# Decode block, backward pass: slab products ordered behind store copies on VectorE, and the forward output stored in the last attention pass

## Chip, cores and metric

One NeuronCore of one Trainium2 chip runs the program; nothing is exchanged with other cores. The metric is the device time of one execution in microseconds (us): the median of three runs, with the lowest and the highest beside it. One further execution is recorded by the hardware profiler; every duration, wait and order below comes from it.

The engines are named as the profile names them: PE is TensorE (matmuls and transposes; PEld its weight loads), DVE is VectorE, ACT is ScalarE, POOL is GpSimd, SP is SyncE. In this kernel SP issues all loads from memory and POOL all stores. Each engine runs its own instruction stream in order.

## What is computed

The reference is a model of four layers applied to one token, and all its gradients. A is attention over a cache of 65,536 positions (32 query heads in 4 groups, head size 128), B a dense layer with a squared relu; both are applied twice with the same weights and the same cache:

```python
x = x + A(layernorm(x), k_cache, v_cache, wq, wo)     # L1
x = x + B(layernorm(x), w1, b1, w2, b2)               # L2
x = x + A(layernorm(x), k_cache, v_cache, wq, wo)     # L3
x = x + B(layernorm(x), w1, b1, w2, b2)               # L4
out, vjp = jax.vjp(f, A_x, A_k_cache, A_v_cache, A_wq, A_wo, B_w1, B_b1, B_w2, B_b2)
grads = vjp(grad_out)
return out, *grads
```

All data are bfloat16. K and V cache are 67 MB each (4 x 65,536 x 128), and so are their gradients. The ten outputs are the forward result `out_0` (1024 values), the gradient of x (`out_1`), of K and V (`out_2`, `out_3`), of wq, wo, w1, b1, w2, b2 (`out_4` to `out_9`).

## The kernel before

**Stages.** The cache is read four times. Pass 1 and pass 2 are the forward attention of L1 and L3 (`attn_fwd`), pass 3 is the first half of L3's backward attention (`attn_bwd3`, softmax gradient and the gradient of the queries), and pass 4, the last, is `attn_bwd4`: the backward attention of L1, and the K and V gradients of L1 and L3 together. Between the passes stand dense stages for the weights; the last of them, called dense34, runs after pass 3 with a PSUM layout of its own.

**The last pass.** `attn_bwd4` goes over 256 items of 8 x 128 cache rows, in 4 groups of 64. `pipeline` (L840) calls, item by item, the steps of the pass, each with its lag: `vT` turns 8 blocks of V on PE and evacuates them to `kt` (L1345, L1348), up to 16 items ahead; `vS` multiplies them with dO (L1382) and forms X on DVE (L1403); `eIn`, `eT` and `xT` turn the saved probabilities and X (L1354, L1360); `dV8` and `dK8` make rows of the V and K gradients; `k8` multiplies K by X for the query gradient (L1457). The K load of a block is written at its first use, the V load at its turn (`kv8`, L365).

**Store copies.** `dV8` and `dK8` call `outer16` (L1418): twice, two matmuls into `ps_gg` (two buffers; L1426), then an evacuation (`evac`, L1430) of 128 x 1024 numbers into a 1 MB staging slot. After two such calls the slot is stored by POOL (L1432). `evac` (L150) puts each copy on ACT (L161) or on DVE (L164), whichever has less written work by its own counts. These evacuations are the "store copies" of this text.

**Background work.** Each item ends with `bg.step` (L862), which advances one piece of other work. Two urgent kinds take the product of a weight matrix with a vector in row form, `g_dO` and `g_dn`, both through `g_rowdots` (L577). It goes over 8 slabs of 128 x 1024 numbers of wo or wq, loaded four at a time as one 1 MB slot (L462): for each slab, DVE multiplies the slab by a vector spread over all partitions (the slab product, L598, into one of the two buffers of `mv_t`), and one step later ACT sums the product along its rows (`total`, L587). Twelve such sets of four products fall into pass 4. The other kind, `bg.normal`, writes the weight gradients as outer products (`rank2`, L1504), paced by a count: a step is taken while the number done is under `bg.total` times the share of items gone. After three big outer products comes `g_biases`, which stores the gradients of b2 and b1.

**Slots.** Loads and staging share an arena of 20 slots of 1 MB, of which up to 8 hold saved probabilities until their group is done. Which slot each load gets is fixed as the program is written; the load then waits for the slot's last user.

**Order of the instructions.** Passes 1 to 3 are written under `tc.manual_schedule`: PE, DVE and ACT run in the text's order. Dense34 and pass 4 are not: there the planner of the framework orders each engine's stream at build time. It runs a model of the program, and each engine takes, of the instructions that are ready in that model, the one that is first in the text. An instruction whose inputs the model holds to be there early is thus put ahead of earlier-written ones that are not yet ready. The stream is then fixed, and on the chip an engine waits at each instruction until its inputs are there.

**The forward output.** In dense34 the second dense layer's w2 is gone through once for the gradient and, beside it (`side_x4`, L1849), for the forward result. After the last slab, `side_x4` adds the bias and the residual on DVE into `x4` (1024 values as 128 x 8) and calls `col_to_dram` (L202): a transpose to 8 rows on PE (L205), a copy to bfloat16 on DVE (L207), and a store of 2 KB issued by POOL (L208).

Of the kernel before, what the change touches and what calls it, by code (L numbers as in the profile page):

```python
# [3 lines left out]

# [9 lines left out]
ALU = mybir.AluOpType  # L14
# [6 lines left out]
def kernel(  # L21
# [24 lines left out]
    nc = tc.nc  # L46
    D = A_x.shape[-1]
    G = A_k_cache.shape[1]
# [3 lines left out]
    HQ = QD // DH  # L52
    R = HQ // G
    F = B_w1.shape[1]
    DC, FC = D // P, F // P
# [38 lines left out]
    def ps_gg():  # L94
        return PS["pool"].tile([P, 1024], F32, name="ps_gg", tag="gg", bufs=2)
# [4 lines left out]
    def ps_mv(shape, dtype=F32):  # L100
        if PS["pass4"]:
            return ps_tr(shape, dtype)
        return PS["pool"].tile(shape, dtype, name="ps_mv", tag="mv", bufs=1)
# [41 lines left out]
    def add_load(act=0.0, dve=0.0, pe=0.0):  # L145
        load["act"] += act
        load["dve"] += dve
        load["pe"] += pe

    def evac(out, in_, kind="bf"):  # L150
        n = 1
        for d in in_.shape[1:]:
            n *= d
        ca = 0.17 + n * 0.00083
        cd = 0.13 + n * (0.00105 if kind == "f32" else 0.00054)

        if PS["pass4"] and kind == "bf":
            ca += 1.5
        if kind == "kta" or kind != "kt" and load["act"] + ca <= load["dve"] + cd:
            load["act"] += 0.17 + n * 0.00083  # L160
            nc.scalar.copy(out=out, in_=in_)  # L161
        else:
            load["dve"] += cd
            nc.vector.tensor_copy(out=out, in_=in_)  # L164


    def col_from_dram(v1d, n, name):
        nj = n // P
        rows = tmp.tile([nj, P], BF, name="rows_c", tag="rows_c")
        nc.sync.dma_start(out=rows[:], in_=v1d.rearrange("(j p) -> j p", p=P))  # L170
        pt = ps_mv([P, nj], BF)
        nc.tensor.transpose(pt[:, :], rows[:, :], ident_b[0:nj, 0:nj])
        col = vec.tile([P, nj], F32, name=name)
        nc.vector.tensor_copy(out=col[:], in_=pt[:])
        return col
# [26 lines left out]
    def col_to_dram(col, n, v1d):  # L202
        nj = n // P
        pt = ps_mv([nj, P], F32)
        nc.tensor.transpose(pt[:, :], col[:, :], ident_f[:, :])  # L205
        rows = tmp.tile([nj, P], BF, name="rows_c", tag="rows_c")
        nc.vector.tensor_copy(out=rows[:], in_=pt[:])  # L207
        nc.gpsimd.dma_start(out=v1d.rearrange("(j p) -> j p", p=P), in_=rows[:])  # L208
# [227 lines left out]
    def d_cols(ap, nb):  # L436
        return ap[:, nb * P:(nb + 1) * P]
# [66 lines left out]
    def w2_slabs(ahead=1):  # L504
        v = f_rows_of(B_w2)
        return slabs("s_w2", lambda k, kn: v[:, k // 4, :, :], FC, 4, D, ahead)
# [52 lines left out]
    def g_bcast_vec(vcol, nj):  # L559
        pt = ps_mv([nj, P], F32)  # L560
        nc.tensor.transpose(pt[:, :], vcol, ident_f[:, :])
        yield
        rows = tmp.tile([32, P], BF, name="bc_rows")
        nc.vector.tensor_copy(out=rows[0:nj, :], in_=pt[:, :])
        vbc = mvs.tile([P, nj * P], BF, name="vbc", tag="vbc", bufs=1)
        yield
        for j0 in range(0, nj, 4):
            pg = ps_gg() if PS["pass4"] else ps_tr([P, 512], F32)
            for jj in range(4):
                nc.tensor.matmul(pg[:, jj * P:(jj + 1) * P], lhsT=ident_b[0:nj, j0 + jj:j0 + jj + 1].to_broadcast([nj, P]),  # L570
                                 rhs=rows[0:nj, :], start=True, stop=True)
            nc.scalar.copy(out=vbc[:, j0 * P:(j0 + 4) * P], in_=pg[:, 0:512])
            add_load(act=0.6)
            yield
        return vbc

    def g_rowdots(slab_it, nk, vcol, nj, finish, name):  # L577
        n = nj * P
        y = vec.tile([P, nk], F32, name=name)
        nc.gpsimd.memset(y[:], 0.0)  # L580
        vbc = None
        due = None
        steps = 8 if PS["pass4"] else WAIT_STEPS

        def total(t, kc):
            def f():
                nc.scalar.activation(out=t[:, :], in_=t[:, :], func=ACTF.Copy, accum_out=y[:, kc:kc + 1])  # L587
            return f
        for kc, slab in slab_it:
            if vbc is None:  # L590
                vbc = yield from g_bcast_vec(vcol, nj)
                for _ in range(steps - WAIT_STEPS + 1):
                    yield "wait"
            elif kc % 4 == 0:
                for _ in range(steps):
                    yield "wait"
            t = mvs.tile([P, n], BF, name="mv_t", tag="mv_t", bufs=2)
            nc.vector.tensor_tensor(out=t[:, :], in0=slab, in1=vbc[:, :], op=ALU.mult)  # L598
            add_load(dve=0.1 + n * 0.00054, act=0.42 + n * 0.00083)
            if due is not None:  # L600
                due()
            due = total(t, kc)
            yield
        due()
        yield
        r = finish(y[:, :])
        if r is not None:
            yield from r
        yield
# [382 lines left out]
    def g_dn(L, dn, g, first):  # L992
        yield from g_rowdots(wq_slabs(g)[0], DC, L["dqT"][:, gsl(g)], R, dn_finish(dn, first), "%s_dn%d" % (L["name"], g))
# [295 lines left out]
    def attn_bwd4(p, La, Lb, on_group, bg, stack, end=()):  # L1289
# [128 lines left out]
        def outer16(name, out, key, xt, gg, j1):  # L1418

            if j1 == 0:  # L1420
                state[key] = Slot(name, True)
            stg = state[key].t[:, :].rearrange("p (j d) -> p j d", d=DH)
            for m in range(2):
                pg = ps_gg()
                for h in range(2):
                    nc.tensor.matmul(pg[:, 512 * h:512 * h + 512], lhsT=xt[64 * h:64 * h + 64, j1 // 8 + m, :],  # L1426
                                     rhs=gg[64 * h:64 * h + 64, :, :].rearrange("p a b -> p (a b)"),
                                     start=True, stop=True, tile_position=(64 * h, 0))
                jj = j1 + 8 * m
                evac(stg[:, jj:jj + 8, :].rearrange("p j d -> p (j d)"), pg[:, :], kind="f32")  # L1430
            if j1 + 16 == J:
                nc.gpsimd.dma_start(out=out, in_=stg)  # L1432
                state.pop(key).free(stored=True)

        def dV8(g, c8):
            b, j0 = divmod(c8, J)
            if 2 * j0 < J:
                outer16("gstv", half(GVv, g, b), "stv", state[("xe", g, b)], state[("GG", g, c8 // SU)][1], 2 * j0)
# [131 lines left out]
    def n_outer(nA, nB, wide=False):  # L1570
        return -(-nB // 8) + nA // 4 + nA * (-(-nB // 8)) if wide else 1 + nA // 4 * 5
# [56 lines left out]
    bg = Background()  # L1628
# [39 lines left out]
    bg = Background()  # L1668
# [146 lines left out]
    bg = Background()  # L1815
# [30 lines left out]
    x4 = vec.tile([P, DC], F32, name="x4")  # L1846
    ps_x4 = ps_acc([P, DC, 64])

    def side_x4(kc, slab):  # L1849
        for nb in range(DC):  # L1850
            nc.tensor.matmul(ps_x4[:, nb, :], lhsT=d_cols(slab, nb), rhs=L4["gb"][:, kc:kc + 1].to_broadcast([P, 64]),
                             start=kc == 0 and nb == 0, stop=kc == FC - 1 and nb == DC - 1, skip_group_check=True)
        add_load(pe=DC * 0.03)
        if kc == FC - 1:
            f = tmp.tile([P, DC], F32, name="ffn_f")
            nc.vector.tensor_tensor(out=f[:], in0=ps_x4[:, :, 0], in1=b2c[:], op=ALU.add)
            nc.vector.tensor_tensor(out=x4[:], in0=x3[:], in1=f[:], op=ALU.add)
            col_to_dram(x4, D, out_0.rearrange("a b d -> (a b d)"))
    rows.add(w2_slabs()[0], FC, DC, lambda: dx2[:], fin_dh2, mix=True, side=side_x4)
    rows.add(w1_slabs()[0], DC, FC, lambda: dh2[:], fin_dx1, cols=f_cols, mix=True)  # L1860
    rows.add(wo_slabs(firstg[3])[0], R, DC, lambda: dx1[:], dO_finish(L1, firstg[3]), inplace=True)
# [10 lines left out]
    bg = Background()  # L1872
# [1 line left out]
    bg.normal.append(g_outer(bgpool, out_8, FC, DC, [L4["g"], L2["g"]], [gx, dx2], a_f=True))  # L1874
    bg.normal.append(g_outer(bgpool, out_5, HQ, DC, [L3["oT"], L1["oT"]], [dx3, dx1]))
    bg.normal.append(g_outer_wide(bgpool, out_6, DC, FC, [L4["n"], L2["n"]], [dh4, dh2]))
    bg.total = 2 + n_outer(FC, DC) + n_outer(DC, FC, True) + n_outer(HQ, DC) + (G - 1) * n_outer(DC, DC)
    bg.steps = len(ITEMS[3]) - 4
    dn1 = vec.tile([P, DC], F32, name="dn1")

    def g_biases():
        gb2 = tmp.tile([P, DC], F32, name="gb2")
        nc.vector.tensor_tensor(out=gb2[:], in0=gx[:], in1=dx2[:], op=ALU.add)
        col_to_dram(gb2, D, out_9)
        yield
        gb1 = tmp.tile([P, FC], F32, name="gb1")
        nc.vector.tensor_tensor(out=gb1[:], in0=dh4[:], in1=dh2[:], op=ALU.add)
        col_to_dram_f(gb1, F, out_7)
        yield
# [66 lines left out]
```

## Time and profile before

| | us |
|---|---|
| median of 3 runs (lowest to highest) | 1946.26 (1945.61 to 1947.33) |
| profiled execution, its own time | 1939.92 |
| its span | 1938.1 |
| PE busy / DVE busy / ACT busy in the span | 1585.2 / 1170.3 / 1044.9 |
| memory traffic: read, written | 617.62 MB, 165.69 MB, 404 GB/s over the span |

By stretches (from the windows of the trace; lengths and busy times in us; the DMA share is the mean busy share of the 16 DMA engines):

| stretch | what | PE | DVE | ACT | PEclk | DMA share | GB/s |
|---|---|---|---|---|---|---|---|
| 1110 to 1210 | dense34, start of pass 4 | 87.6 | 68.7 | 55.7 | 0.95 | 0.85 | 310 |
| 1210 to 1485 | pass 4 | 238.9 | 200.9 | 196.2 | 0.88 | 1.01 | 418 |
| 1485 to 1500 | pass 4 | 8.9 | 11.8 | 9.3 | 0.77 | 0.95 | 391 |
| 1500 to 1660 | pass 4 | 138.0 | 123.7 | 119.7 | 0.94 | 1.01 | 422 |
| 1660 to 1690 | pass 4 | 17.6 | 13.4 | 13.2 | 0.66 | 0.77 | 307 |
| 1690 to 1770 | pass 4 | 73.8 | 59.7 | 59.3 | 0.91 | 1.01 | 417 |
| 1770 to 1785 | pass 4 | 5.3 | 5.6 | 4.7 | 0.66 | 0.93 | 365 |
| 1785 to 1880 | pass 4 | 89.9 | 79.8 | 75.4 | 1.00 | 1.01 | 418 |
| 1880 to 1898 | last loads | 7.3 | 5.1 | 5.0 | 0.72 | 1.02 | 424 |
| 1898 to 1938 | end | 29.0 | 26.1 | 24.6 | 0.86 | 0.84 | 337 |

How to read it: an engine's busy time counts its instructions alone; what it waits for shows as idle time, which the profile puts down to the one whose signal came last ("<-PE ps_gg L1426" is a wait for the matmul of L1426 into `ps_gg`; "<-issue" is one for which it finds no such signal). PEclk is the clock granted to TensorE, as a share of the full one. A DMA share of 1 says that the DMA engines were never empty. In the timeline a line gives start and length, engine, line, operation, output <- input and shapes, and in brackets the idle time ahead of it.

### The profile page before, as it was taken

Reading aid. Unit: us, or ns where it says so; the run is one execution under the profiler, and the core shown is the slowest. Engines: PE = TensorE matmul, PEld = TensorE weight load, DVE = VectorE, ACT = ScalarE, POOL = GpSimd, SP = SyncE. Lnnn points to the kernel's source line nnn. Section 1 sums busy time; section 2 is a strip of 40 time slices with the busy share of each in tenths; the row PEclk is TensorE's granted clock in tenths of the full one; section 3 lists DMA queues with packets and bytes.
Section 4 is the critical chain, followed back from the end, with each engine's and each line's share of the span. In section 5 each row is a group of like instructions: output and inputs, shape, how many; then the busy total and the mean of one; then the engine's idle time right before and its main releaser. Section 6 shows DMA issues by size and latency. Waiting matters only on the chain. (4 is left out here: it accounts for less than half of the span.)

```text
span 1938.1 us, 66986 instructions
## 1 busy us (share of the span) xinstructions
PE 1585.2 (82%) x30199; PEld 1301.4 (67%) x30199; DVE 1170.3 (60%) x2453; ACT 1044.9 (54%) x1617; POOL 142.2 (7%) x321
## 2 busy tenths in 40 slices
PE   6878778688777888977787898889997987697987
PEld 6878777678777877877776886555554654454554
DVE  5655555255555554545454567777775886685876
ACT  3444334245433545445363455766875885575775
POOL 0000000000000000000000001121111211121211
PEclk9999899689999999998899999898997998797998
DMA  9999999999999998999999988999999999899998
GB/s 393 427 425 425 429 427 415 391 407 423 427 425 429 428 422 309 377 425 429 426 424 421 408 314 308 425 424 389 425 424 413 419 424 424 345 419 397 424 422 352
DMA packets 107149, 787.63 MB, mean 406 GB/s; under 512 B 9440, under 2 KB 16622, under 8 KB 42222
## 3 DMA queue, kind: packets, MB, share of 16 engines
q1 hardware_dynamic: 82782, 617.65, 77.2%
q0 software_dynamic: 24080, 165.70, 20.5%
q8 instruction: 236, 3.87, 0.7%
q14 instruction: 51, 0.42, 0.1%
HBM read 617.62 MB, written 165.69 MB: 404 GB/s over the span
## 5 line engine op out<-in xcount | busy, mean ns | idle before, releaser
L164 DVE COPY kt<-ps_tr 128x1024 bf16<-128x1024 bf16 x724 | 496.3, 688 | 429.0 <-PE ps_tr L1024 244.0
L161 ACT CAST arena<-ps_gg 128x1024 bf16<-128x1024 f32 x457 | 444.4, 1011 | 185.0 <-PE ps_gg L1426 137.9
L1024 PE MATMUL ps_tr<-ident_b,arena 128*128 128x128 bf16 x3840 | 308.2, 225 | 36.9 <-DMA arena<-in_A_k_cache_dram 27.5
L161 ACT COPY kt<-ps_tr 128x1024 bf16<-128x1024 bf16 x164 | 171.0, 1046 | 186.1 <-PE ps_tr L1216 103.3
L164 DVE CAST arena<-ps_gg 128x1024 bf16<-128x1024 f32 (+2 forms) x186 | 222.2, 1195 | 77.1 <-PE ps_gg L1426 34.5
L1024 PEld LDWEIGHTS <-arena 128*128 128x128 bf16 x3840 | 232.9, 101 | 44.7 <-DMA arena<-in_A_k_cache_dram 30.3
L1126 PE MATMUL ps_acc<-arena 128*128 128x64 bf16 (+4 forms) x4096 | 205.6, 196 | 60.2 <-DMA arena<-in_A_v_cache_dram 45.1
L1426 PE MATMUL ps_gg<-GG,xt 64*128 64x512 bf16 x1024 | 210.6, 409 | 43.3 <-DVE arena L164 28.3
L1345 PE MATMUL ps_tr<-ident_b,arena 128*128 128x128 bf16 x1824 | 177.4, 232 | 33.7 <-DMA arena<-in_A_v_cache_dram 30.7
L1126 PEld LDWEIGHTS <-arena 128*128 128x128 bf16 x4096 | 159.9, 100 | 66.1 <-DMA arena<-in_A_v_cache_dram 48.7
L1042 PE MATMUL ps_sc<-L_qpad,kt 128*128 128x64 bf16 (+7 forms) x3584 | 183.0, 194 | 16.3 <-issue 8.3
L1107 ACT ACTIVATE arena<-S_sb,L_negm 128x128 bf16<-128x128 f32 x256 | 165.5, 1002 | 55.7 <-DVE L_negm L1092 42.2
L1216 PE MATMUL ps_tr<-ident_b,arena 128*128 128x128 bf16 x1920 | 154.3, 226 | 44.3 <-DMA arena<-in_A_v_cache_dram 43.5
L1345 PEld LDWEIGHTS <-arena 128*128 128x128 bf16 x1824 | 116.8, 103 | 90.7 <-issue 55.2
L1042 PEld LDWEIGHTS <-kt 128*128 128x128 bf16 x3584 | 152.6, 100 | 20.2 <-issue 8.8
L1216 PEld LDWEIGHTS <-arena 128*128 128x128 bf16 x1920 | 117.1, 101 | 48.8 <-DMA arena<-in_A_v_cache_dram 46.1
L1457 PEld LDWEIGHTS <-arena 128*128 128x128 bf16 x2048 | 92.2, 101 | 57.8 <-issue 39.9
L1107 ACT ACTIVATION_READ_ACCUMULATOR arena<-S_sb,L_negm 128x1 f32 x256 | 127.9, 500 | 0.0
L1426 PEld LDWEIGHTS <-xt 64*128 64x128 bf16 x1024 | 64.5, 94 | 90.1 <-issue 52.3
L587 ACT ACTIVATE mv_t<-mv_t 128x1024 bf16<-128x1024 bf16 x96 | 102.1, 1065 | 35.8 <-DVE mv_t L598 35.8
L1382 PE MATMUL ps_sc<-DOB,kt 128*128 128x64 bf16 (+3 forms) x1824 | 112.3, 197 | 0.1
L1270 PE MATMUL ps_acc<-dsT,arena 128*128 128x64 bf16 (+7 forms) x2048 | 103.1, 194 | 11.3 <-DMA arena<-in_A_k_cache_dram 7.8
(317 smaller groups left out, 2154.0 us busy)
## 6 DMA issues: line engine op xcount, KB each, us to landing
arena<-in_A_k_cache_dram SPq DMA_DIRECT2D x82, 2048.0 KB, 21.7
arena<-in_A_v_cache_dram SPq DMA_DIRECT2D x79, 2048.0 KB, 21.7
out_dram<-arena POOLq DMA_DIRECT2D x149, 1024.0 KB, 16.2
arena<-in_A_v_cache_dram SPq DMA_DIRECT2D x84, 1024.0 KB, 14.2
arena<-in_A_k_cache_dram SPq DMA_DIRECT2D x84, 1024.0 KB, 14.6
arena<-in_A_wo_dram SPq DMA_DIRECT2D x22, 1024.0 KB, 19.6
arena<-in_B_w_dram SPq DMA_DIRECT2D x21, 1024.0 KB, 9.2
arena<-in_A_wq_dram SPq DMA_DIRECT2D x18, 1024.0 KB, 18.0
```

The costliest lines, as they stand in the source:

```text
L161: nc.scalar.copy(out=out, in_=in_)
L164: nc.vector.tensor_copy(out=out, in_=in_)
L587: nc.scalar.activation(out=t[:, :], in_=t[:, :], func=ACTF.Copy, accum_out=y[:, kc:kc + 1])
L1024: nc.tensor.transpose(pt[:, i, :], kb8[:, i, :], ident_b[:, :])
L1042: nc.tensor.matmul(state["ps_s"][:, s:s + w, :].rearrange("p a b -> p (a b)"), lhsT=kt[:, i, :], rhs=L["qpad"][:, g, 0:w, :].rearrange("p ...
L1107: nc.scalar.activation(out=E(p, g, c0, SU)[:, :, h], in_=S[:, h, :], func=ACTF.Exp, bias=L["negm"][:, g, su, h:h + 1], scale=SCALE, accum_ ...
L1126: nc.tensor.matmul(ps_o[:, 0:w, :], lhsT=vb8[:, i, :], rhs=E(p, g, c, w), start=(c % SU == 0), stop=(c % SU == SU - 1), skip_group_check=True)
L1216: nc.tensor.transpose(pt[:, i, :], vb8[:, i, :], ident_b[:, :])
L1270: nc.tensor.matmul(ps_dq[:, 0:w, :].rearrange("p a b -> p (a b)"), lhsT=kb8[:, i, :], rhs=dsT[:, s:s + w, :].rearrange("p a b -> p (a b)") ...
L1345: nc.tensor.transpose(pt[:, i, :], vb8[:, i, :], ident_b[:, :])
L1382: nc.tensor.matmul(state["ps_dp"][:, s:s + w, :].rearrange("p a b -> p (a b)"), lhsT=vt[:, i, :], rhs=DOB[:, g, 0:w, :].rearrange("p a b - ...
L1426: nc.tensor.matmul(pg[:, 512 * h:512 * h + 512], lhsT=xt[64 * h:64 * h + 64, j1 // 8 + m, :], rhs=gg[64 * h:64 * h + 64, :, :].rearrange(" ...
```

## The change

`mark_store_copy`, called after each evacuation of `outer16`, notes that instruction if it went to DVE. `behind_store_copy` wraps the slab product of `g_rowdots` and, once such a copy has been noted, makes the planner put the product behind the last noted one on DVE: an edge of order between two instructions of the same engine, without a semaphore. In passes 1 to 3 nothing has been noted yet, and the wrapper does nothing.

The store of `x4` leaves `side_x4` and becomes the first of now three steps of `g_biases`, so it runs as background work of the last pass, after the three big outer products; `bg.total` counts one step more. In the last pass `col_to_dram` takes its PSUM buffer from the two of `ps_tr`, as it does there for the other rows.

```diff
+    PIN = {"copy": None}
+
+    def mark_store_copy():
+
+        i = nc.cur_bb.bb.instructions[-1]
+        if i.engine == mybir.EngineType.DVE:
+            PIN["copy"] = i
+
+    @contextmanager
+    def behind_store_copy():
+
+        if PIN["copy"] is None:
+            yield
+        else:
+            with tc.issue_after(PIN["copy"]):
+                yield
...
             t = mvs.tile([P, n], BF, name="mv_t", tag="mv_t", bufs=2)
-            nc.vector.tensor_tensor(out=t[:, :], in0=slab, in1=vbc[:, :], op=ALU.mult)
+            with behind_store_copy():
+                nc.vector.tensor_tensor(out=t[:, :], in0=slab, in1=vbc[:, :], op=ALU.mult)
...
                 evac(stg[:, jj:jj + 8, :].rearrange("p j d -> p (j d)"), pg[:, :], kind="f32")
+                mark_store_copy()
...
             nc.vector.tensor_tensor(out=x4[:], in0=x3[:], in1=f[:], op=ALU.add)
-            col_to_dram(x4, D, out_0.rearrange("a b d -> (a b d)"))
...
-    bg.total = 2 + n_outer(FC, DC) + n_outer(DC, FC, True) + n_outer(HQ, DC) + (G - 1) * n_outer(DC, DC)
+    bg.total = 3 + n_outer(FC, DC) + n_outer(DC, FC, True) + n_outer(HQ, DC) + (G - 1) * n_outer(DC, DC)
...
     def g_biases():
+        col_to_dram(x4, D, out_0.rearrange("a b d -> (a b d)"))
+        yield
         gb2 = tmp.tile([P, DC], F32, name="gb2")
```

## The prediction

> **What bounds the kernel now.** I read the page first, then what VectorE (DVE) waits for in the last pass, then the timeline around its longest waits, then the DMA share in short windows there, then SyncE's queue, last the dense stage ahead of the pass. All times are microseconds of the profiled execution.
>
> ```profile
> span 1938.1 us, 66986 instructions
> DMA  9999999999999998999999988999999999899998
> GB/s 393 427 425 425 429 427 415 391 407 423 427 425 429 428 422 309 377 425 429 426 424 421 408 314 308 425 424 389 425 424 413 419 424 424 345 419 397 424 422 352
> ```
>
> A slice is 48.5 us. Most run at 424 GB/s with the DMA engines full: memory traffic bounds the kernel, and time is lost only where the rate dips. Slices 23 and 24 (counted from 0; 1114 to 1211) are the dense stage and the start of the last pass; slices 34 and 36 lie within the last pass, where DVE waits like this (1470 to 1800; in total, times, longest):
>
> ```profile
> DVE mv_t L598 <- issue: 27.8, 3, 14.0
> DVE mv_t L598 <- DMA arena<-in_A_wq_dram: 5.5, 1, 5.5
> ```
>
> L598 is the slab product. Four times, 33.3 us in all, DVE stands in front of one whose slab has not landed. The longest, on DVE's timeline and then SyncE's:
>
> ```profile
> 1660.72 0.42 DVE L164 COPY xt<-ps_tr 128x512 bf16<-128x512 bf16 x1
> 1675.15 0.69 DVE L598 TENSOR_TENSOR mv_t<-arena,vbc 128x1024 bf16<-128x1024 bf16 x1 [14.02 <-issue]
> 1675.76 1.22 DVE L164 CAST arena<-ps_gg 128x1024 bf16<-128x1024 f32 x1
> ```
>
> ```profile
> 1655.77 0.38 SPq L462 DMA_DIRECT2D arena<-in_A_wq_dram  x1
> 1656.24 1.00 SPq L365 DMA_DIRECT2D arena<-in_A_v_cache_dram  x1
> 1657.55 24.26 SPq L365 DMA_DIRECT2D arena<-in_A_k_cache_dram  x2
> 1685.40 2.17 SPq L365 DMA_DIRECT2D arena<-in_A_v_cache_dram  x3
> ```
>
> The slab's load is issued at 1655.77 and lands about 1675.1, 19 us later, behind what was queued. Meanwhile the evacuations behind the product wait, TensorE (PE) stops for its PSUM buffers (12.2 us on L1426, by the waits), no K or V slot comes free, and SyncE issues nothing between 1657.6 and 1681. The queued transfers run out (windows: length, busy times, clock, DMA share, GB/s):
>
> ```profile
> 1668.00:1672.00 4.00, 0.00 (x0) 0.00 (x0) 0.00 (x0) 0.00 (x0) 0.00 (x0) 0.50 0.93 391
> 1672.00:1676.00 4.00, 0.00 (x0) 0.00 (x0) 0.85 (x2) 0.12 (x1) 0.00 (x0) 0.50 0.25 104
> 1676.00:1680.00 4.00, 2.97 (x23) 1.50 (x22) 3.77 (x5) 2.84 (x4) 0.53 (x1) 0.50 0.28 102
> 1680.00:1684.00 4.00, 4.00 (x43) 2.49 (x43) 3.15 (x7) 2.06 (x3) 0.00 (x0) 0.50 0.80 270
> ```
>
> That is 4 x (0.07 + 0.75 + 0.72 + 0.20) = 7.0 us of empty DMA engines from a 14.0 us stall; half of it comes after the product, while PE runs at a granted clock of 0.50. The 10.1 us stall before 1778.34 costs 1.2 us in the same way (share 0.39 in 1780 to 1782), the 5.5 us one before 1485.5 costs 0.8 (share 0.62 in 1496 to 1498), the 3.7 us one before 1577.6 nothing (share 1.01 throughout). Sum 9.0. A stall is thus free for as long as queued transfers last.
>
> **Part 1, the products' place.** In the last pass the planner orders DVE; it has put products far ahead of where the text writes them. Pairing the 2401 computing instructions of DVE in the trace with the program's, one by one, gives each product's place in both orders. For all 48 products of the pass, the last store copy written ahead of it on DVE comes 6 to 59 instructions after it, 4 to 43 us. For the four stalled ones it comes at 1513.5, 1603.9, 1707.8 and 1806.9. Take the stall itself out of these times, and they still lie 18 to 23 us after the slab had landed (1707.8 - 14.0 - 1675.1 = 18.7 for the longest). Behind those copies a product finds its slab there. All four stalls should go, and with them the 9.0 us; the products themselves stay (48 x 0.68 us), only later. The wait moves to nobody on DVE; ScalarE's summing of each product (L587, which waited 26.4 us for products in this pass) follows later, and nothing urgent hangs on the sums: the rows dO they make are finished at 1276.7, 1433.6 and 1616.8 (L948), and the next group's matmuls first read them at 1332.0, 1527.7 and 1718.0 (L1382), 55 us later or more.
>
> What does hang on them is the slab's slot. In eleven of the twelve sets of four products, the next writer of that slot is a load (K or V in ten sets, a slab in two) issued within 0.7 us of the fourth product's end, in the twelfth 2.4 us after it. The hold of the slot grows by the same span. The moved load has a lead over its first use now: 17.2 us in the first set (K issued 1229.5, used 1246.6), 36.5 in the second (V, 1246.6 and 1283.1), 16.8 and 36.0 in the next two, 22 to 50 later. The copies that the fourth products get bound to lie at 1245.9, 1282.9, 1403.2 and 1436.9, so with 2 us for the copy and the product these four leads shrink to nothing, nothing, 5 and 5 us, under the median from issue to landing, 13.3 for V and 16.0 for K; in the later sets 12 to 22 us stay. One 1 MB load fewer in flight is 1.05 MB / 424 GB/s = 2.5 us of cover. Bounds: 0 (issued bytes less landed bytes, loads and stores together, are 2.0 MB at 1246 and 3.6 at 1282, so a missing one leaves the engines fed; also the loads freed later were ones that ran ahead of more urgent ones) and 4 x 2.5 = 10. I take one, 2.5, since 1310 to 1330 is already short: 0.1 MB of loads are open at 1310 and the share falls to 0.77.
>
> **Part 2, the last output.** Its row turn now stands in the dense stage, in PE's order:
>
> ```profile
> 1144.79 0.28 PE L682 MATMUL ps_tr<-ident_b,arena 128*128 128x128 bf16 x2
> 1147.22 0.27 PE L205 MATMUL ps_mv<-ident_f,x 128*8 128x128 f32 x1 [2.15 <-DVE x L1857]
> ```
>
> PE waits 2.15 us for x4, which DVE reaches behind four 1.22 us products of the stage, then turns it in 0.27; DVE loses 0.28 and 0.37 around its copy and then stands 2.70 us for PE. From 1110 to 1210 the DMA share is 0.85, so the stage's end follows PE. Gain 2.15 + 0.27 = 2.4; bounds 0 (something else late in the stage, slab loads are waited for from 1164 on) and 2.4 + 0.65 = 3.1. I take 2.4. In the last pass the same three instructions cost what the bias row's do there: 0.27 on PE, 0.27 on DVE, 0.53 of issue on GpSimd with 2 KB. DMA is full there (share 1.01 from 1785 to 1880), which hides them; uncovered it would be 0.6. GpSimd is past its limit nowhere (21.8 busy of those 95), and stores queued behind this small one lose half a microsecond out of the 17 they take. It needs one PSUM turning buffer of two for about 0.6 us. The pacing total 150 to 151 shifts background steps by less than one item: nothing.
>
> Sum: -9.0 - 2.4 + 2.5 = -8.9. The profiled execution took 1939.9 around its span of 1938.1; the median of the three runs is 1946.3, 6.3 above it, in which the same stalls must lie. I set the difference against the median: 1937.4.
>
> **Rivals.** A, the held slots decide: PE runs in order, and where a moved K or V load has no lead it stands until the landing, 14 us in the first two sets and about 8 in the next two. Priced by the stalls seen, 7.0 each for 14 us and 1.2 for 8 to 10, that is 16.4 lost against 11.4 gained: +5.0, 1951.3. For it: the load follows the product in every set, and in the first group only six or so slots turn over K and V. Against: the planner sees the later release and orders PE's other work ahead, and V runs up to 16 items ahead of its use. It decides once more than two sets fall under the landing time with less than 2 MB queued. The Trainium skill (Perfetto Trace Analysis, Optimization Strategy) says that a gap repeating on the engine that should be full can mean too little buffer space for the next tile; this trace shows no such repeated gap on DMA before the change, and the rule would speak for A.
>
> B, DVE's stalls go and the span does not follow: the planner's new order runs into the DMA a little further on (PE already waits 30.7 us for V loads in this pass), or slabs land behind the copies too. Then only the dense stage's 2.4 stays: 1943.9. Against: the empty DMA time has the stall's own place. The Trainium skill (Perfetto Trace Analysis, Identifying the Most-Contended Engine) says to work on the engine that is busiest, which is DMA here, not DVE at 60%; by it alone the change would bring about B's time.
>
> C, more is given back. By rate instead of share, the rows of ten microseconds at 1490, 1500, 1670, 1680, 1690 and 1780 (374, 395, 155, 343, 378, 297 GB/s) fall short of 424 by 1.2 + 0.7 + 6.3 + 1.9 + 1.1 + 3.0 = 14.2; with 2.4 and no slot cost -16.6: 1929.7. Against: 1690 to 1700 has a share of 1.00, so part of it is slow stores.
>
> **How the numbers follow.** Forecast 0.50, A 0.18, B 0.12, C 0.20. This kernel's time tells a change from none at about 0.2%, 3.9 us. Faster: the forecast and C but for a little, 0.67. Same: B and the forecast's edge, 0.14. Slower: A with a new order's bad luck, 0.19. Range: C's side with all slot costs absent and the dense bound, 1926; A's side with a microsecond over, 1952. The forecast's own range is 1931 to 1942.
>
> **What would show it.** Right: no wait of DVE in front of L598 over 1 us in the last pass; DMA share at 1 from 1210 to the last loads; the x4 turn gone from PE's dense order and that stage about 2.4 shorter. Wrong: K or V waits of PE before 1300 that empty the DMA (A), or a full share with a span unchanged (B).

## The result, and the profile after

| | before | after |
|---|---|---|
| median of the runs on one chip (lowest to highest) | 1946.26 (1941.79 to 1947.67) | 1965.33 (1960.70 to 1966.40) |
| ratio, 95% interval | 1 | 1.0097 (1.0081 to 1.0112) |
| span of the profiled execution | 1938.1 | 1958.7 |
| waits of DVE in front of the slab product, last pass | 33.3 in four | 0.2 in one |
| waits of PE for K and V loads, 1210 to the end | 46.6 in 14 | 92.0 in 16 |
| from the last matmul of pass 3 to dx1 on DVE | 53.0 | 51.0 |

The change made the kernel 1% slower: 1965.33, outside the range of 1926 to 1952 and on the other side of 1946.26. (The lines of the code moved down by 17 to 19: the product is L616 now, the store copies' matmul L1444, the turn of V L1363, the K matmul L1476, the K and V loads L382, the slab loads L479.)

The lines of the page that answer to those of before, span, DMA share and rate in 40 slices of 49 us:

```profile
span 1958.7 us, 66950 instructions
DMA  9999999999999998999999988999999999999996
GB/s 395 426 427 426 427 428 409 399 406 425 427 426 426 429 420 293 402 427 425 426 426 416 393 322 336 393 374 410 425 409 412 406 425 417 374 413 376 416 422 247
```

The deepest dip of before within the pass, slice 34, is shallower (374 for 345), but slice 36 is deeper (376 for 397), slices 25 and 26, which ran at 425 and 424, are at 393 and 374, and the last has fallen from 352 to 247. The rate is lost elsewhere, and the end is longer.

What DVE waits for in front of a product, from 1210 on (total, times, longest), has gone as predicted:

```profile
DVE mv_t L616 <- ACT mv_t L604: 0.2, 1, 0.2
```

What PE waits for in the same stretch, first after, then before:

```profile
PE ps_tr L1363 <- DMA arena<-in_A_v_cache_dram: 50.1, 7, 12.1
PE ps_acc L1476 <- DMA arena<-in_A_k_cache_dram: 41.9, 9, 9.0
...
PE ps_gg L1444 <- DVE arena L164: 2.5, 5, 1.3
```

```profile
PE ps_tr L1345 <- DMA arena<-in_A_v_cache_dram: 30.7, 10, 10.7
PE ps_gg L1426 <- DVE arena L164: 28.3, 8, 12.2
PE ps_acc L1457 <- DMA arena<-in_A_k_cache_dram: 15.9, 4, 10.7
```

PE's waits for DVE's copies were the stalls of the products, passed on; they fell from 28.3 to 2.5. Its waits for data grew by 45.4, nearly twice as much. One of these in full, the second set of products. DVE's timeline around the set's last product, then SP's, then PE's:

```profile
1279.11 1.22 DVE L164 CAST arena<-ps_gg 128x1024 bf16<-128x1024 f32 x1
1280.25 0.68 DVE L616 TENSOR_TENSOR mv_t<-arena,vbc 128x1024 bf16<-128x1024 bf16 x1
```

```profile
1277.88 0.33 SPq L382 DMA_DIRECT2D arena<-in_A_k_cache_dram  x1
1280.45 0.83 SPq L382 DMA_DIRECT2D arena<-in_A_v_cache_dram  x2
1287.63 0.33 SPq L382 DMA_DIRECT2D arena<-in_A_k_cache_dram  x1
```

```profile
1301.21 0.29 PE L1363 MATMUL ps_tr<-ident_b,arena 128*128 128x128 bf16 x1 [12.08 <-DMA arena<-in_A_v_cache_dram]
```

The fourth product ends at 1280.9. In that instant the second of the two V loads at 1280.45 is issued, into the slot which the slab leaves. It is what PE needs next: PE has run out of V at 1289.1 and stands 12.1 us until it lands. Before, the same load left at 1246.6 with 36.5 us to spare. The windows from 1288 on show what a standing PE costs (busy times of PE, PEld, DVE, ACT, POOL, then clock, DMA share, GB/s):

```profile
1288.00:1292.00 4.00, 1.14 (x18) 0.66 (x15) 3.14 (x9) 1.11 (x2) 1.15 (x2) 1.00 1.01 424
1292.00:1296.00 4.00, 0.00 (x0) 0.00 (x0) 0.00 (x0) 0.00 (x0) 0.00 (x0) 0.53 1.01 428
1296.00:1300.00 4.00, 0.00 (x0) 0.00 (x0) 0.00 (x0) 0.00 (x0) 0.00 (x0) 0.50 1.01 426
1300.00:1304.00 4.00, 2.79 (x18) 1.41 (x19) 0.41 (x1) 1.85 (x2) 0.00 (x0) 0.50 1.01 426
1304.00:1308.00 4.00, 3.99 (x38) 2.13 (x39) 3.05 (x6) 2.67 (x4) 0.53 (x1) 0.76 0.54 223
1308.00:1312.00 4.00, 3.77 (x62) 2.51 (x61) 3.96 (x13) 3.44 (x5) 1.63 (x4) 1.00 0.62 262
1312.00:1316.00 4.00, 3.62 (x51) 2.34 (x49) 4.00 (x7) 2.85 (x4) 0.00 (x0) 1.00 0.90 285
```

While PE stands, the DMA engines are full: the wait itself costs no transfer time. But a standing PE frees no slot, and SP issues nothing, so the engines run empty once PE is back: 4 x (0.46 + 0.38 + 0.10) = 3.8 us lost. That is the mechanism by which the prediction priced DVE's stalls, now with PE waiting for a load in DVE's place. Not every stand is followed by empty engines: counted in the same way, in windows of 4 us, 2.1 us are lost behind the stand that ends at 1257, 3.1 behind that of 1689 and 4.1 behind that of 1792, and next to nothing behind those that end at 1420, 1466, 1590, 1647 and 1752.

By stretches, the transfer time missing to 424 GB/s, (424 - rate) / 424 x length, from the windows of both kernels, first before, then after:

```profile
1210.00:1290.00 80.00, 70.08 (x887) 44.15 (x884) 62.38 (x111) 57.46 (x71) 15.25 (x28) 0.87 1.01 424
1290.00:1330.00 40.00, 31.15 (x352) 18.99 (x349) 24.18 (x46) 23.03 (x26) 7.37 (x15) 0.83 0.97 395
1330.00:1470.00 140.00, 125.15 (x1545) 78.47 (x1544) 105.97 (x194) 105.87 (x124) 24.97 (x48) 0.90 1.01 420
1470.00:1700.00 230.00, 186.43 (x2464) 120.29 (x2462) 166.09 (x299) 159.49 (x197) 38.66 (x75) 0.89 0.98 403
1700.00:1880.00 180.00, 159.57 (x2108) 100.90 (x2103) 136.25 (x233) 131.95 (x150) 36.77 (x67) 0.93 1.01 416
```

```profile
1210.00:1290.00 80.00, 64.84 (x801) 39.54 (x797) 57.33 (x99) 56.23 (x69) 13.93 (x26) 0.85 0.98 402
1290.00:1330.00 40.00, 27.67 (x328) 16.91 (x329) 25.10 (x51) 22.26 (x24) 6.07 (x12) 0.83 0.90 352
1330.00:1470.00 140.00, 112.41 (x1448) 71.65 (x1445) 98.09 (x182) 96.95 (x114) 24.64 (x47) 0.90 1.01 419
1470.00:1700.00 230.00, 191.85 (x2524) 123.00 (x2522) 167.52 (x299) 160.26 (x194) 41.56 (x76) 0.89 0.99 409
1700.00:1880.00 180.00, 157.69 (x2016) 98.58 (x2014) 132.44 (x227) 129.07 (x153) 34.84 (x65) 0.89 0.99 402
```

| stretch | before: GB/s, missing | after: GB/s, missing | difference |
|---|---|---|---|
| 1210 to 1290 | 424, 0.0 | 402, 4.2 | +4.2 |
| 1290 to 1330 | 395, 2.7 | 352, 6.8 | +4.1 |
| 1330 to 1470 | 420, 1.3 | 419, 1.7 | +0.4 |
| 1470 to 1700 (three of the four old stalls) | 403, 11.4 | 409, 8.1 | -3.3 |
| 1700 to 1880 | 416, 3.4 | 402, 9.3 | +5.9 |

Up to 1880 the change loses 11.3 us more. The span grew by 20.6; the other 9.3, and the 3 us by which the pass began sooner (dx1 at 1170.9 for 1174.0), fall in the end of the pass. PE stands there again at 1894.9 for 9.0 us waiting for a K load, which the chain of waits of after leads through (DMA takes up 7% of the span in that chain). But before stands there too, 10.7 us from 1881.5 on, also for a K load; what differs is what comes behind the stand:

```profile
1898.00:1959.00 61.00, 42.23 (x460) 25.06 (x460) 29.89 (x54) 27.27 (x29) 7.60 (x12) 0.67 0.70 280
```

The granted clock is 0.67 there, for 0.86 in the last 40 us of before. From 1904 to 1922 PE works without a pause at 0.50; before, it was back at 0.99 from 1896 on. The DMA share is 0.70: PE's remaining work sets the end. This is one execution of each kernel; in that of e1 below, with the products bound as well, the clock was back 3.9 us after the stand.

### The profile page after: what moved, and what is told of

Read it like the earlier page. It is cut to its first block, busy times and chain, and to the rows that moved or that the text cites. A ratio compares the mean times of both kernels' runs of the same rounds, so it can differ in the third digit from the quotient of the medians.

```text
span 1958.7 us, 66950 instructions
## 1 busy us (share of the span) xinstructions
PE 1585.2 (81%) x30199; PEld 1295.7 (66%) x30199; DVE 1171.3 (60%) x2451; ACT 1045.1 (53%) x1619; POOL 144.9 (7%) x321
## 5 line engine op out<-in xcount | busy, mean ns | idle before, releaser
L164 DVE CAST arena<-ps_gg 128x1024 bf16<-128x1024 f32 (+2 forms) x190 | 227.2, 1196 | 100.1 <-PE ps_gg L1444 61.1
L1042 PEld LDWEIGHTS <-arena 128*128 128x128 bf16 x3840 | 231.2, 100 | 45.4 <-DMA arena<-in_A_k_cache_dram 33.6
L1444 PE MATMUL ps_gg<-GG,xt 64*128 64x512 bf16 x1024 | 211.8, 414 | 20.0 <-ACT arena L161 8.9
L1363 PE MATMUL ps_tr<-ident_b,arena 128*128 128x128 bf16 x1824 | 179.5, 234 | 52.9 <-DMA arena<-in_A_v_cache_dram 50.1
L1363 PEld LDWEIGHTS <-arena 128*128 128x128 bf16 x1824 | 118.6, 104 | 110.4 <-issue 57.0
L1060 PEld LDWEIGHTS <-kt 128*128 128x128 bf16 x3584 | 151.9, 100 | 22.1 <-ACT kt L161 10.5
L1476 PEld LDWEIGHTS <-arena 128*128 128x128 bf16 x2048 | 89.9, 101 | 81.7 <-issue 44.8
L1476 PE MATMUL ps_acc<-X,arena 128*128 128x64 bf16 (+3 forms) x1536 | 95.3, 198 | 33.3 <-DMA arena<-in_A_k_cache_dram 33.3
L1400 PEld LDWEIGHTS <-kt 128*128 128x128 bf16 x1824 | 83.0, 101 | 42.9 <-issue 41.3
```

What stands on the lines that cost most here:

```text
L1042: nc.tensor.transpose(pt[:, i, :], kb8[:, i, :], ident_b[:, :])
L1060: nc.tensor.matmul(state["ps_s"][:, s:s + w, :].rearrange("p a b -> p (a b)"), lhsT=kt[:, i, :], rhs=L["qpad"][:, g, 0:w, :].rearrange("p ...
L1363: nc.tensor.transpose(pt[:, i, :], vb8[:, i, :], ident_b[:, :])
L1400: nc.tensor.matmul(state["ps_dp"][:, s:s + w, :].rearrange("p a b -> p (a b)"), lhsT=vt[:, i, :], rhs=DOB[:, g, 0:w, :].rearrange("p a b - ...
L1476: nc.tensor.matmul(ps_dq[:, 0:w, :].rearrange("p a b -> p (a b)"), lhsT=kb8[:, i, :], rhs=X[:, s:s + w, :].rearrange("p a b -> p (a b)"), ...
```

## The experiments

Each ratio is against runs of the kernel before on the same chip, taken between the others; the intervals are 95%. H stands for the held slots, the prediction's rival A.

| run | what | ratio (interval) |
|---|---|---|
| e1_pin_only | binding alone | 1.0084 (1.0068 to 1.0100) |
| e2_x4_only | moved output alone | 1.0027 (1.0017 to 1.0036) |
| e3_hold_only | products in their old place, slots held as long as in the change | 1.0155 (1.0140 to 1.0170) |
| e4_third_last | whole change, bound behind the third last store copy | 1.0077 (1.0054 to 1.0100) |
| e7_wait5 | whole change, five steps between sets for eight | 1.0054 (1.0033 to 1.0074) |
| e5_pin_ring | whole change, slabs in staging slots | 1.0055 (1.0036 to 1.0074) |
| e6_ring_only | nothing bound, slabs in staging slots | 1.0078 (1.0062 to 1.0094) |
| e9_own_slots | whole change, two slots for slabs alone | 1.0016 (1.0001 to 1.0031) |
| e10_own_unbound | nothing bound, two slots for slabs alone | 0.9999 (0.9988 to 1.0010) |
| e11_own_pin_only | binding alone, two slots for slabs alone | 0.9991 (0.9979 to 1.0003) |
| e8_step_only | an empty step where the output would be | 1.0012 (1.0000 to 1.0025) |
| e12_x4_merged | moved output, no step of its own | 0.9989 (0.9976 to 1.0001) |
| e13_hold_own | as e3, two slots for slabs alone | 1.0069 (1.0047 to 1.0091) |
| e14_shift64 | kernel before, slots 64 bytes further on | 1.0062 (1.0046 to 1.0078) |
| e15_hold_in_place | as e3, slots not moved | 1.0107 (1.0087 to 1.0128) |
| e16_hold_own_in_place | as e13, slots not moved | 0.9992 (0.9981 to 1.0003) |

**Each part alone: e1, e2.** e1 is the change with the output's store back in `side_x4`; e2 is the kernel before with only that store moved into `g_biases`, with its own `yield` and the total raised by one.

> The binding of the slab products alone; the last output is stored in the dense stage as before. Theory H (held slots: the products now free their 1 MB slab slot later, the K or V load that goes into it is issued later, and PE stands for it): all of the loss is here, so about 1.010 to 1.013 of the time of before, that is the change's 1.0097 plus the 2 to 3 us that moving the output gives in the dense stage; PE's waits for K and V loads in the last pass stay near 92 us (before 47). Theory X (the moved output disturbs the last pass): without the move the binding gives what was forecast, about 0.995, and those waits are back near 47 us.

> The last output moved alone, products as before. Theory H: the dense stage ends 2 to 3 us earlier and nothing else changes much, 0.997 to 0.9995. Theory X: slower, about 1.01.

The binding is the loss: 0.84% of the 0.97%. Its execution has no stall of DVE, and PE waits 89.6 us for K and V, as H had it; H's number for e1 counted on a gain from moving the output and is missed. The moved output costs 0.27%, between H's number and X's, where a gain was expected; e8 and e12 below take that up.

**The hold without the binding: e3.** The products stay where the planner puts them, and a copy of two columns of each set's fourth slab is bound in their stead, so that the slot is let go as late as in the change:

```diff
+            if PS["pass4"] and kc % 4 == 3:
+                held = tmp.tile([P, 2], BF, name="slab_held")
+                with behind_store_copy():
+                    nc.vector.tensor_copy(out=held[:, :], in_=slab[:, 0:2])
```

> The kernel before, products where they were, plus one tiny DVE copy (two columns) out of the fourth slab of each set, bound behind the store copy as in the change, so that each slab slot is held as long as in the change while no product moves. The small copies' results go nowhere. Theory H: the DVE stalls of 33 us stay and PE's waits for K and V rise well over 47 us, so the time is no better than the change's: 1.008 to 1.02. Rival O (what costs is the new place of the products and the order that the planner makes around them, not the slot): holding costs next to nothing, 0.999 to 1.002.

Slower by 1.55%, more than the whole change. But in its profiled execution passes 1 to 3, whose text is that of before, were 13.5 us longer as well (last matmul at 1134.6, before 1121.1). So it couldn't stand by itself; e13 to e16 settle it.

**A shorter hold: e4, e7.** e4 keeps the last three store copies on DVE and binds behind the oldest; e7 sets `steps = WAIT_STEPS`, five, in `g_rowdots`.

> The whole change, but each product is bound behind the third last store copy on DVE instead of the last one, so it may run some 11 us earlier. Theory H: the slots are held less long; PE's waits for K and V fall between 47 and 92 us, DVE stalls at products stay under 10 us, and the time comes out under the change's: 0.994 to 1.004. Rival O: binding makes the planner's order worse wherever the copy stands, about 1.008 to 1.01.

> The whole change with five steps instead of eight between a set of products and the next, so that each bound set is written, and its slot handed on, some steps sooner after its load. H: hold falls from 58 us towards 45, time 1.000 to 1.006. O: 1.007 to 1.011, as the change. If the products come before their data (waits on DVE again, 10 us or more), it says nothing of either.

From a slab's load to the issue of the next writer of its slot pass 44.8 us on the mean of the twelve sets before, 58.4 after. e4 brought this only to 56.1, and the time moved little: H's number is missed and the rival's nearly met, but with the slots held almost as long the run hardly tells the two apart. e7 brought it to 52.2, and nearly half of the loss went, as H had it, if at the upper end of its numbers. Hold and time go together, but two points don't make a proof.

**Other slots for the slabs: e5, e6.** A slab's load takes a slot of the ring in which the gradients are staged. No K or V load has a slab's slot next any more; e5 has the change, e6 nothing bound.

```diff
-                sl = Slot(name)
+                sl = Slot(name, fill=PS["pass4"])
```

> The whole change, and in the last pass a slab is loaded into a slot of the ring in which the gradients are staged, so that no K or V load has a slab's slot. Theory H (the binding is paid for by the K and V loads that wait for a slab's slot): the 17 us of later loads are gone and the 33 us of waiting products stay gone; PE's waits for K and V in the last pass fall from 92 to 45 us or less, time 0.990 to 1.000 of before. Rival O (the new order of DVE's work costs by itself, whoever has the slot): 1.005 to 1.012, PE's waits for K and V 80 us or more. Rival R (the ring is too small: staging copies and stores now wait for the products): above 1.012, with waits of ACT or DVE in front of the copies into the staging slots.

> The kernel before with the same choice of slots and nothing bound: the control to the run above. H: 0.996 to 1.002, since the slots were handed on early enough before (mean hold 45 us); products still wait 30 us on DVE. If it is below 0.996, the slab slots cost time already before the change. O: 0.998 to 1.002. R: above 1.004.

Neither kernel met H's number, and PE's waits for K and V in e5, 68.4 us, lie between H's and O's. By itself e5's time would speak for the rival that blames DVE's new order; but the control e6, with the old order, is the slower one. Its 1.0078 is what R expected of it, though not in R's way: SP's queue shows the wait. First e6, then e5 (waits of SP, 1200 to 1940):

```profile
SPq L462 <- DMA out_dram<-arena: 117.6, 11, 26.9
```

```profile
SPq L479 <- DMA out_dram<-arena: 126.0, 10, 22.7
```

A slab's load now waits until the ring slot has been stored to memory, in front of SP's other loads: at 1858.80 in e5 SP issues a slab load after standing 22.7 us, and three K and V loads leave behind it within 4 us. The wait was moved from one user of the slots to all of them. Still, with the slots as they are in both, the bound kernel is faster by 0.0023, though it carries the moved output as well and the two intervals overlap: products wait 47.0 us on DVE in e6 and 5.4 in e5, and binding them seems to return something.

**Slots of their own: e9, e10, e11.** The two planes that the first group's saved probabilities leave are kept for slabs, which take them by turns; the first two sets use a ring slot. A slab's load then waits for nothing but the products of the set before the last.

```diff
-                sl = Slot(name)
+                sl = Slot(name, fill=PS["pass4"], at=OWN.popleft() if PS["pass4"] and OWN else None)
+                sl.own = PS["pass4"] and sl.i in (plane(0, firstg[3]), plane(1, firstg[3]))
...
-                if not sl.users:
+                if sl.own and not sl.users:
+                    OWN.append(sl.i)
+                elif not sl.users:
                     sl.free()
...
+                if PS["pass4"] and g == firstg[3]:
+                    OWN.append(plane(lay, g))
+                    continue
                 RING.add(plane(lay, g))
```

> The whole change; in the last pass the slabs go by turns into two slots of their own (the planes that the first group's scores leave), the first two sets into a slot of the ring. No K or V load and no staged output uses a slab's slot, and a slab's load waits for the products of the set before the last one alone. Theory H (the binding gains what the products waited, and loses more because the longer held slots stand in the way of K and V loads): the kernel is level with or below its control, the run below, by 0.2 to 0.6%, and 0.993 to 1.001 of before; PE's waits for K and V 35 to 55 us; no SP wait at the slab's load for a store. Rival O (the order of DVE's work costs by itself): 1.005 to 1.012 and above its control.

> The kernel before with the same slots, nothing bound: the control. H: 0.996 to 1.004, with the 30 us of waiting products back; if the ring's stores, which held SP for 118 us at the slabs' loads in the run with ring slots, were what made that one 1.0078, this one is below it by 0.4% or more. O: 0.998 to 1.002 and below the run above.

> Own slots and bound products, the last output stored in the dense part as before. H, with the plan's shift by the moved output costing 0.1 to 0.3%: 0.990 to 0.999, the fastest of the three. If the moved output costs nothing here: as the whole change with own slots, within 0.1%.

e9 is above H's number and above its control, e10 is where H had it, e11 at the edge. e9 and e11 differ in the moved output alone, by 0.0025, which is taken up below. The binding's 0.84% is gone: 0.9991 in e11 for 1.0084 in e1, with the products bound in the same way and the slots taken still longer (84.9 us on the mean, since the slabs are loaded earlier). What differs is who has the slot next, and with it how early the slabs come. PE's waits for data in e11:

```profile
PE ps_acc L1483 <- DMA arena<-in_A_k_cache_dram: 28.3, 9, 6.3
PE ps_tr L1370 <- DMA arena<-in_A_v_cache_dram: 26.8, 7, 8.6
```

55.1 us, none over 8.6, for 92.0 in the change. But e11 isn't told apart from before, nor from its control e10, so the gain of 9.0 doesn't appear either. In e10 the products wait 9.3 us in one stall, because slabs with slots of their own are loaded earlier: the slots took most of the stalls away without the binding. And though the last K or V load of e11 leaves at 1894.2 (before 1903.1), its span ends at 1944.0 (before 1938.1): 50 us behind that load for 35 before. What the transfers gained in this execution came back as work of PE left over at the end (51.3 us of it from 1880 on, 36.3 before).

**The moved output: e8, e12.** e8 puts a bare `yield` at the head of `g_biases` of the kernel before and raises the total by one, and leaves the output in dense34. e12 moves the output, but into the step that stores the gradient of b2, with no step more.

> The kernel before with one empty step at the head of the biases' generator and the total raised by one, the output left where it was: the moved output's place without the output. If moving the output costs because it shifts the plan of everything behind it in the last pass: 1.002 to 1.004, as the moved output alone (1.0027). If the output's own work there costs: 0.999 to 1.001.

> The kernel before with the last output turned and stored in the last pass, in the step that already turns and stores the first bias gradient, so that the plan has no further step. If the moved output costs because its own step and the raised total shift the plan: 0.998 to 1.001, and a gain of up to 2.4 us from the shorter dense part shows. If the output's own work in the last pass costs (its place in PE's and DVE's order): 1.002 to 1.004, as with its own step (1.0027).

The moved output costs nothing without a step of its own (0.9989), and the empty step alone costs 0.12%, between the two numbers expected and about half of e2's cost (its interval touches 1). That points at the shift of the plan by a step rather than at the output; in the pair e9 and e11 output and step together cost 0.0025 again. Where the other half of it comes from, and how one step costs anything, isn't settled. The gain of 2.4 us isn't shown either way: 0.9989 is 2.1 us, and the interval reaches 1.

**The hold again: e13 to e16.** The tile of e3's two-column copy had moved the 20 slots from byte 48896 of each partition to 48960. e13 repeats e3 with slots of their own; e14 is the kernel before with an unused tile of 64 bytes there; e15 and e16 are e3 and e13 with the copy written into a tile that existed already (`tag="rows_c"`), so that the slots are back at 48896.

> The kernel before with the two-column copy of each set's fourth slab bound behind the store copy (the hold alone, 1.0155 with the slots of before), and slabs in two slots of their own. H (a held slot costs only through the K and V loads that have it next): 0.998 to 1.003, as the unbound kernel with own slots (0.9999). If the bound copy itself or something in the passes ahead made the 1.0155: 1.008 to 1.016 again.

> The kernel before with an unused tile of 64 bytes a partition ahead of the slots, so that these begin at byte 48960 of a partition instead of 48896, as they do in both kernels with the two-column copy; nothing else differs. If the shift is what made their first three passes 11 to 13 us longer: 1.005 to 1.009, with 421 to 424 GB/s in the stretches of those passes where the kernel before has 426 to 427. If not: 0.998 to 1.002 at 426 GB/s.

> The hold alone with the slots of before, the copy written to a tile that was there, so that the slots begin where they did. H: 1.006 to 1.010 (the 16 us that its last pass was longer, less what is chance). If the hold costs nothing and all of the 1.0155 was the shift: 0.998 to 1.002.

> The hold alone with slots of its own, the slots beginning where they did. H and the shift: 0.998 to 1.003, as the unbound kernel with own slots (0.9999). If the bound copy itself costs: 1.005 to 1.009.

e13 missed both numbers, and e14 says why: 64 bytes cost 0.62% by themselves. With the slots in place the answer is plain: holding alone costs 1.07%, a little over what H had, with the slots of before and nothing with slots of their own (0.9992). PE's waits for data are 76.8 us in e15 and 29.6 in e16. This is H by itself, with no product moved. The stretches of single executions agree: from dx1 to the end e15 takes 780.4 us, e16 763.4 and before 764.1; e13, with the slots shifted, takes 764.7, and its loss lies ahead of dx1 (1188.5 for 1174.0).

No version beats the kernel before by more than can be told: e11, e12 and e16 lie at 0.9989 to 0.9992, with 1 in every interval.

## Why the prediction was wrong

**What bounds the kernel.** Right up to the last loads: transfers, and the time is lost where the engines run empty. Behind them it is PE's remaining work, which the prediction didn't count.

**The products' place.** Right: all four stalls went, and none came in their stead on DVE.

**The step that failed: "I take one, 2.5".** The prediction had the moved loads, their lost leads (to nothing in two sets, 5 us in two), and A's rule that PE stands until the landing; then it took 2.5 us for it, because 2 to 3.6 MB were queued. In the first four sets PE stood 7.3, 12.1, 11.2 and 5.2 us, where A had 14, 14, 8 and 8. The hold alone measures +1.07% (1964.62 for 1942.13, 22.5 us between the medians) where the slot goes to K or V, and nothing where it doesn't. That is nine times the term, and over its bound of 10. The queued megabytes did cover the stand itself, as the windows above show; what they didn't cover is the time after it, when no slot has come free, behind the first two of these four and behind two later ones. The prediction had seen this behind DVE's stalls ("half of it comes after the product") and didn't apply it to PE's.

A had the mechanism and too small a price: +5.0 for +19. It ended with the fourth set, on the ground that 12 to 22 us of lead stay in the later ones. In the change PE stands there too, 6.4 at 1583, 6.5 at 1641, 11.3 at 1677, 4.7 at 1747, 7.3 at 1785 and 9.0 at 1895, at loads whose slot's last user was PE itself: a later PE lets go later. The load for the stand at 1641 stood besides behind a slab load in SP's queue, which had waited 3.3 us for a bound product. Two of the six have their like before, 10.7 us each at 1618 and 1881. The Trainium skill (Perfetto Trace Analysis, Optimization Strategy) says that a gap which repeats on the engine that should be full can be a sign of too little buffer space; the prediction set it aside since it saw no such gap in the trace of before, though its own sum counted three. The trace of after agrees with the page: DMA runs short behind four stands of PE within the pass, and two slots set aside for the slabs take the loss away (e11).

**The term -9.0.** Probably too large, but not settled. Three pairs have like slots, one kernel bound and one not: e11 is 0.0008 below e10, where 9.3 us of stalls were left; e1 is 0.0023 below e15, where 22.7 were; e5 is 0.0023 below e6, where 47.0 were, and e5 carries the moved output with its step, which cost 0.0025 between e9 and e11. The intervals overlap in each pair, and e1 and e15 come from two chips. By an estimate from the last two pairs the stalls were worth some 4 to 9 us. In its place the sum came back in part: 1470 to 1700 got 3.3 us back, where the prediction had counted 7.8, and a new stand of PE lies in that stretch. And pieces of transfer time saved in the middle aren't pieces of span: in e11 the loads end 9 us sooner and the kernel doesn't.

**The term -2.4, and "The pacing total 150 to 151 shifts background steps by less than one item: nothing".** The turn did leave dense34, but no run shows the gain. In the execution after, the stage was 2.0 shorter (51.0 for 53.0), and executions differ by more than that: with the turn in it the stage took 51.3 to 55.1 in eleven kernels, 53.5 on the mean, without it 51.0 to 55.3 in seven, 52.8 on the mean. The step was not nothing: with the moved output in it, it cost 0.25 to 0.27% in two pairs, about 5 us; by itself 0.12% (e8).

**B and C.** B's first half (the stalls go, the span doesn't follow) is what e11 shows at 0.9991, once nothing else is disturbed. The sentence beside it, from the Trainium skill (Perfetto Trace Analysis, Identifying the Most-Contended Engine), to work on the busiest engine, agrees with this: once no stall of DVE was left, e11 was no faster than before. C fell.

## What to carry to other kernels

An instruction that is moved later keeps every buffer that it reads until then: look up who gets the buffer next, and count from that load's first use, not from the moved instruction. Price a wait by what the bounding engine does after it, when the buffers that would have come free are missing, and let a late engine be late further on too. Give a late reader a buffer of its own before moving it (here that took the loss away and brought no gain); and when an experiment adds a tile, see that nothing else moved.

## What was not expected of the hardware

**64 bytes of address cost 0.6%.** e14 adds to the kernel before an unused tile of 64 bytes and the instruction that clears it; what is allocated behind it, the slots above all, begins 64 bytes further on, the slots at 48960 for 48896. In the profiled executions most of the loss lies in the passes ahead: dx1 at 1189.8 for 1174.0, and from there to the end 767.1 us for 764.1. Two stretches of passes 1 and 2, before and then e14 (columns as above):

```profile
150.00:300.00 150.00, 121.48 (x2908) 116.39 (x2905) 81.07 (x182) 63.38 (x154) 0.00 (x0) 0.95 1.01 427
450.00:600.00 150.00, 119.09 (x2951) 114.03 (x2947) 82.94 (x191) 64.87 (x154) 0.00 (x0) 0.99 1.01 426
```

```profile
150.00:300.00 150.00, 120.09 (x2859) 115.02 (x2858) 80.14 (x179) 61.23 (x149) 0.00 (x0) 0.95 1.01 423
450.00:600.00 150.00, 118.61 (x2833) 113.30 (x2830) 79.57 (x180) 62.84 (x152) 0.00 (x0) 0.95 1.01 421
```

With the engines full in both, the rate is 0.9 and 1.2% lower (425 and 422 in a stretch of pass 3, 0.7%). The K and V loads of these passes are 2 MB each, 16 KB in a partition; a packet of 16 KB takes 611 ns before and 613 in e14 at the median, and 0.3 to 0.7% more on the mean, which is only a part of the loss. Where the rest comes from is open, and only this one offset was tried. 48896 is 191 x 256, 48960 is not a multiple of 256. The Trainium skill (DMA: Bandwidth & Descriptors, How a descriptor splits into AXI transactions) says, by the vendor's account, that a descriptor is split into transactions of 256 bytes, that each must start at a multiple of 256, and that one which starts off them fetches some bytes for nothing. For 16 KB an estimate from that page's beats of 32 bytes is 2 more on 512, 0.4%, about what the packets show; whether the rule, which the page gives for reads, holds for writes to the slots isn't shown.

**The clock falls while PE waits.** In the windows from 1288 the granted clock is 0.53 and 0.50 once PE stands, and still 0.50 in the first 2.8 us of its work after 12.1 us of standing. PE comes back at half speed just when it should free slots. How long it stays there varies: behind the stand that ends at 1792 PE works 22 us at 0.50 while the rate falls to 310 GB/s, and behind the last one 18 us at 286. So part of the loss may be the clock's, as a consequence of the stands; how much was not tried. Half clock alone doesn't make a kernel slow: from 1210 to the end of the profiled executions the mean clock is 0.89 before, 0.87 after and 0.86 in e16, which is no slower than before.
